# Hourglass attention and an MoE layer on one core: q and k interleaved token by token, and new prices for the order of work

## The chip, the core and the metric

The kernel runs on one core of a Trainium2 chip. Its time is the device time of one execution in microseconds. The core has five engines with a queue each, and every queue is worked off in order: TensorE (PE, with weight loads shown apart as PEld), VectorE (DVE), ScalarE (ACT), GpSimd (POOL) and SyncE (SP), which here only issues DMAs. Engines wait for each other by semaphores.

## The reference

Eight batches with eight heads, 576 tokens and 64 dimensions go through two attentions, whose outputs are added, and then through a layer with a tanh shrink:

```python
q_d, k_d, v_d = mean over 4 neighbouring tokens of q, k, v          # 144 tokens
out_up = repeat(softmax(q_d @ k_d.T / 8) @ v_d, 4)                   # full attention, pooled
scores = where(abs(i - j) < 4, q @ k.T / 8, -1e9)                    # local attention
out_local = softmax(scores) @ v
x = (out_up + out_local) as [4608 tokens, 8 heads * 64]
h = x @ w_in                                                         # 512 -> 2048
out = (h - tanh(h)) @ w_out                                          # 2048 -> 512
```

Inputs and output are float32; the kernel computes its matmuls in bf16.

## The kernel before

**Attention by pairs of heads.** The function `attention(p)` builds the work of one pair of heads; there are 32 pairs (p = 0 to 31), four to a batch. Per pair: q and k are loaded into `qkn` (two DMAs), with q on even and k on odd partitions; a cast to bf16 sorts them into `qr` (L447 on GpSimd for p >= 4); then they are transposed, so that the head dimension lies on partitions, and copied to `qk`. For p < 16 the transpose is nine matmuls on TensorE into PSUM (L477) and one ScalarE copy of 1,152 elements (L481). For p >= 16 (`T_DMA`) it is a DMA transpose `qT` issued by SP (L464) and two ScalarE copies of 576 elements, one for q, one for k (L468). `qk` is a tile of 1,192 columns: 576 of q, nine zeros, 576 of k from column `KOFF` = 585, and 31 zeros.

Two additions pool groups of four tokens (`half` L492, `qkd` L497). Local scores are eight matmuls L511 for token blocks 0 to 3 and two for block 4, each of 128 k columns against 120 (96) q columns of one head; pooled scores are four matmuls L534. Exponentials run on ScalarE (L552, L563, L566), band masks on VectorE (L556 for 960 columns, L570 for 192). Eighteen output matmuls (L581, L588) follow, then reciprocal and normalising on VectorE (L600, L602). For p < 16 the result is transposed back on TensorE (L612 to L616) and joined on VectorE (L643). For p >= 16 it is transposed by a DMA `lT` (L619) and joined (two operations, L626 and L632) on VectorE or GpSimd, whichever the planner picks. The pooled v of p >= 16 is made on GpSimd (L402, L406).

**The MoE part** works on nine blocks of 512 tokens. `mm1` (L663) makes a 128 x 512 tile of h from four matmuls, ScalarE the tanh (L671), VectorE the difference `gT` (L674). `mm2` (L690) makes 128 rows of output from sixteen matmuls; ScalarE copies them to `y` (L701), SP stores them (L704). There are 576 matmuls of each kind. Four PSUM tiles `ps_hy` are shared by both. A block needs all four pairs of every batch that it touches.

**The order** is made by a planner, the class `Program`. Each operation is recorded with an engine, an assumed duration in ns, what it reads and writes, and a priority. `order()` plays this through: whichever engine is free first takes the ready operation with the lowest priority number. Attention has 10 * p; MoE matmuls have 5000, so they fill what time is left on TensorE. Operations with a choice of engines take the one that is free first in the plan. The instructions are emitted in the planned order, and the chip then runs each engine's queue in that order, whatever the real durations are. `slack` is an extra delay that the planner may assume before an operation.

Of the kernel before, what the change touches and what calls it, by code (L numbers as in the profile page):

```python
# [184 lines left out]
def kernel(  # L185
# [18 lines left out]
    A9 = 9  # L204
# [4 lines left out]
    KOFF = 585  # L209
# [27 lines left out]
    qk = fixed("qk", [128, 1192], BF16, 2)  # L237
    qT = fixed("qT", [128, A9, 128], BF16, 2)
    half = fixed("half", [128, 2, G, 2], FP32)
# [193 lines left out]
    def attention(p):  # L433
# [8 lines left out]
        cold = 1.5 if p < NP else 1.0  # L442

# [8 lines left out]
        for h in range(2 if p < NEARLY else 0):  # L452
# [3 lines left out]
                      for eng, ns, fn in REORDER[h]],  # L456
# [4 lines left out]
        full = bass.AP(tensor=qk[s].tensor, offset=qk[s].offset,  # L461
                       ap=[qk[s].ap[0], [KOFF, 2], [1, 576]])
        if p >= T_DMA:
# [3 lines left out]
            for i in range(2):  # L467
                op("ACT", 600, lambda i=i: A.copy(  # L468
                    out=full[:, i].rearrange("p (g a) -> p g a", a=A9),
                    in_=qT[s].rearrange("p a (g i) -> p i g a", i=2)[:, i]),  # L470
                   reads=[("qT", s)], writes=[("qk", s, i)], pri=pri)
        else:
            b16 = ps.rearrange("p n c -> p (n c)").bitcast(BF16)[:, 0:2 * S]

            def tr():
# [3 lines left out]
            op("PE", 520 * cold, tr, reads=[("qr", s, 0), ("qr", s, 1), "ident"],  # L479
               writes=ts, pri=pri)  # L480
            op("ACT", 1240, lambda: A.copy(  # L481
                out=full.rearrange("p i (g a) -> p i g a", a=A9),
                in_=b16.rearrange("p (a g i) -> p i g a", a=A9, i=2)),
               reads=ts,
               writes=[("qk", s, 0), ("qk", s, 1)], pri=pri)


        four = full.rearrange("p i (g a) -> p i g a", a=4)
        adders = ADDERS[p >= NEARLY]

        def add1(eng):
            eng.tensor_tensor(out=half, in0=four[:, :, :, 0:2],  # L492
                              in1=four[:, :, :, 2:4], op=ALU.add)

        def add2(eng):
            with nc.allow_low_precision("pooled q and k"):
                eng.tensor_tensor(out=qkd[s][:, 0:2 * G].rearrange("p (i g) -> p i g", i=2),  # L497
                                  in0=half[:, :, :, 0],
                                  in1=half[:, :, :, 1], op=ALU.add)
        P.choice([(name, n1, lambda eng=eng: add1(eng)) for name, n1, _, eng in adders],  # L500
                 reads=[("qk", s, 0), ("qk", s, 1)], writes=["half"], pri=pri)
# [6 lines left out]
        def score(t, hh, c, sc=sc):  # L508
            rows = slice(64 * hh, 64 * hh + 64)
            k0 = KOFF + QW * t - 4  # L510
            T.matmul(sc[:, c:c + NQ[t]], qk[s][rows, k0:k0 + 128],  # L511
                     qk[s][rows, QW * t:QW * t + NQ[t]], start=p >= NP, stop=p >= NP or t >= 3)
# [27 lines left out]
        qks = [("qk", s, i) for i in range(2)]  # L540
# [3 lines left out]
        if new:  # L544
            op("PE", 620, s12, reads=qks + [("qkd", s)], writes=ts + ox, pri=pri)
        else:
            op("PE", 420 * cold + 600 * (p < NP), s1,
               reads=qks + ["bias"] * (p < NP), writes=ts, pri=pri)
# [3 lines left out]
        op("ACT", 870, lambda: A.activation(  # L552
            out=e1, in_=ps[:, :, 0:480], func=AF.Exp, scale=SCALE),
           reads=ts, writes=[("E", e, 0)], pri=pri)
        if p >= NP:
            op("DVE", 850, lambda: V.tensor_tensor(  # L556
# [4 lines left out]
        if not new:  # L561
            op("PE", 380 * cold + 150 * (p < NP), s2, reads=qks + [("qkd", s)], writes=ts, pri=pri)
        op("ACT", 240, lambda: A.activation(  # L563
            out=e2v, in_=ps2[:, :, 0:96], func=AF.Exp, scale=SCALE),
           reads=ts2, writes=[("E", e, 1)], pri=pri)
        op("ACT", 560, lambda: A.activation(  # L566
            out=e3, in_=ps2[:, :, 96:384], func=AF.Exp, scale=SCALE / 16.0),
           reads=ts2, writes=[("E", e, 2)], pri=pri)
        if p >= NP:
            op("DVE", 300, lambda: V.tensor_tensor(  # L570
# [24 lines left out]
        op("PE", 570 * cold, outs,  # L595
# [6 lines left out]
        op("DVE", 1010, lambda: V.tensor_tensor(  # L602
# [15 lines left out]
        if p >= X_DMA:  # L618
# [18 lines left out]
            P.choice([("DVE", 850, lambda: join(V)), ("POOL", 1450, lambda: join(GP))],  # L637
                     reads=[("lT", s)], writes=[("x", b, j)], pri=pri)
            return
        op("PE", 370 * cold, back, reads=[("ln", s)], writes=ox, pri=pri)  # L640
# [12 lines left out]
    def mm1(kb, fc):  # L653
# [12 lines left out]
        for part in range(2):  # L666
# [4 lines left out]
        op("ACT", 490, lambda: A.activation(  # L671
            out=u[us], in_=ps_hy[slot], func=AF.Tanh),
           reads=[("hy", slot)], writes=[("u", us)], pri=-1)
        op("DVE", 620, lambda: V.tensor_tensor(  # L674
# [195 lines left out]
```

The softmax here doesn't subtract the row's maximum and nothing guards it: scores larger than these inputs give would overflow.

## Time and profile before

| what | value |
|---|---|
| median of 6 runs | 345.47 us (342.51 to 348.68) |
| profiled execution, its own time | 345.01 us |
| its span, first to last instruction | 343.3 us |
| granted TensorE clock, mean | 0.988 |
| TensorE matmuls busy | 327.1 us (95%) |
| VectorE, ScalarE, GpSimd busy | 216.1, 217.1, 162.7 us |
| DMA | 56.52 MB, mean 165 GB/s |

The span is the profiled execution without what lies around it; 1.7 us lie between the two numbers. Slices are fortieths of the span (8.6 us); a digit is a busy share in tenths. A group of instructions has a line, an engine, an operation, output and inputs with their shapes and a count; behind the first bar the busy time in us and the mean duration in ns, behind the second the idle time just before and what ended it. [...] successive matmuls overlap, and their pace is read from several in a row.

### The profile page before, as it was taken

The numbers are of one execution on the slowest core, as the hardware profiler recorded it, in microseconds if no ns is written. First come the engines' busy times: TensorE is split into PE (matmuls) and PEld (weight loads), VectorE is DVE, ScalarE is ACT, GpSimd is POOL, SyncE is SP. The second block draws the span as 40 slices with busy tenths as digits, with TensorE's granted clock in tenths as the row PEclk, the third lists the DMA queues.
The fourth block names the chain that finished last, engine by engine and source line by source line (L and its number), as shares of the span: only waits on it lengthen the run. The fifth ranks groups of instructions, "written<-read, shape, count | busy, mean of one in ns | idle before, by whom it ended". The sixth has DMA issues, their size and how long they took to land.

```text
span 343.3 us, 6637 instructions
## 1 busy us (share of the span) xinstructions
PE 327.1 (95%) x2520; PEld 163.9 (48%) x2520; DVE 216.1 (63%) x341; ACT 217.1 (63%) x350; POOL 162.7 (47%) x191
## 2 busy tenths in 40 slices
PE   7978999999999999997798899999999999999995
PEld 3554555565555554443344445455444444444442
DVE  5784784388877667979988889876433433344300
ACT  3965765679879589986758779875443444344411
POOL 6775448747798629887756889441000000000000
PEclk9998999999999999999989999999999999999999
DMA  7999999998779909999999999322201000100021
GB/s 240 283 220 228 238 279 266 298 307 226 220 187 216 256 31 213 211 217 270 226 241 238 263 233 217 79 70 61 57 32 61 31 32 31 61 31 32 31 87 67
DMA packets 99213, 56.52 MB, mean 165 GB/s; under 512 B 77678, under 2 KB 86382, under 8 KB 99182
## 3 DMA queue, kind: packets, MB, share of 16 engines
q1 hardware_dynamic: 94670, 51.32, 60.5%
q0 software_dynamic: 4224, 4.19, 7.4%
q10 hardware_dynamic: 288, 0.59, 0.5%
q8 instruction: 19, 0.31, 0.4%
q14 instruction: 12, 0.10, 0.1%
HBM read 42.46 MB, written 9.44 MB: 151 GB/s over the span
## 4 chain that ended last, share of the span: by engine, by line
PE 75%; DVE 12%; ACT 6%; DMA 2%; issue 2%; POOL 1%; SPq 0%; ACTq 0%; POOLq 0%; DVEq 0%
PE ps_hy L663 31%; PE ps_hy L690 30%; DVE E L556 4%; PE ps_ox L581 3%; PE ps_ts L511 2%; DVE gT L674 2%; PE ps_ts L477 2%; PE ps_ox L588 2%; DVE xT L632 2%; DVE E L570 2%; ACT E L552 2%; DMA qkn<-in_q_dram 2%; DVE xT L626 2%; PE ps_ox L616 1%; ACT qk L468 1%
## 5 line engine op out<-in xcount | busy, mean ns | idle before, releaser
L663 PE MATMUL ps_hy<-xT,w_in_sb 128*128 128x512 bf16 x576 | 146.8, 383 | 2.2 <-DVE xT L643 1.5
L690 PE MATMUL ps_hy<-w_out_sb,gT 128*128 128x512 bf16 x576 | 144.0, 382 | 0.0
L674 DVE TENSOR_TENSOR gT<-ps_hy,u 128x512 bf16<-128x512 f32 x144 | 96.4, 684 | 73.9 <-ACT u L671 73.2
L671 ACT ACTIVATE u<-ps_hy 128x512 f32<-128x512 f32 x144 | 84.5, 601 | 69.4 <-PE ps_hy L663 68.9
L690 PEld LDWEIGHTS <-gT 128*128 128x128 bf16 x576 | 54.5, 98 | 62.5 <-issue 1.1
L663 PEld LDWEIGHTS <-w_in_sb 128*128 128x128 bf16 x576 | 53.8, 98 | 63.6 <-issue 5.0
L492 POOL TENSOR_TENSOR half<-qk 128x576 f32<-128x576 bf16 x29 | 33.6, 1158 | 30.7 <-ACT qk L481 15.6
L447 POOL CAST qr<-qkn 128x1152 bf16<-128x1152 f32 x28 | 33.5, 1197 | 11.2 <-PE ps_ts L477 5.6
L468 ACT COPY qk<-qT 128x576 bf16<-128x576 bf16 x32 | 38.1, 1215 | 0.0
L556 DVE TENSOR_TENSOR E<-E,mask 128x960 bf16<-128x960 bf16 x28 | 28.3, 1011 | 13.2 <-ACT E L552 12.8
L552 ACT ACTIVATE E<-ps_ts 128x960 bf16<-128x960 f32 x30 | 29.2, 974 | 10.3 <-PE ps_ts L511 10.0
L701 ACT COPY y<-ps_hy 128x512 f32<-128x512 f32 x36 | 21.1, 586 | 19.2 <-PE ps_hy L690 18.7
L602 DVE TENSOR_TENSOR ln<-ps_ox,r 128x896 bf16<-128x896 f32 x30 | 32.7, 1089 | 0.9
L381 POOL CAST vw<-vst 128x640 bf16<-128x640 f32 x32 | 26.1, 816 | 7.0 <-DMA vst<-in_v_dram 5.4
L581 PE MATMUL ps_ox<-vw,E 128*128 128x65 bf16 x300 | 19.4, 194 | 6.3 <-DVE E L570 4.5
L481 ACT COPY qk<-ps_ts 128x1152 bf16<-128x1152 bf16 x14 | 15.7, 1124 | 13.1 <-PE ps_ts L477 11.3
L581 PEld LDWEIGHTS <-E 128*128 128x128 bf16 x320 | 16.1, 98 | 14.1 <-DVE E L570 5.3
L402 POOL TENSOR_TENSOR v<-v 72x512 f32<-72x512 f32 x16 | 20.8, 1303 | 0.9
L497 POOL TENSOR_TENSOR qkd<-half 128x288 bf16<-128x288 f32 x29 | 20.3, 699 | 0.9
L406 POOL TENSOR_TENSOR vp<-v 72x256 bf16<-72x256 f32 x16 | 12.3, 771 | 14.2 <-PE ps_ox L588 13.2
L511 PEld LDWEIGHTS <-qk 64*128 64x128 bf16 x320 | 9.6, 95 | 17.1 <-issue 16.3
L570 DVE TENSOR_TENSOR E<-E,mask 128x192 bf16<-128x192 bf16 x28 | 15.5, 555 | 0.4 <-ACT E L563 0.3
(90 smaller groups left out, 255.2 us busy)
## 6 DMA issues: line engine op xcount, KB each, us to landing
vst<-in_v_dram SPq DMA_DIRECT2D x62, 160.0 KB, 4.9
qkn<-in_q_dram SPq DMA_DIRECT2D x32, 288.0 KB, 5.1
out_dram<-y SPq DMA_DIRECT2D x36, 256.0 KB, 2.0
qkn<-in_k_dram SPq DMA_DIRECT2D x30, 288.0 KB, 4.8
v<-in_v_dram SPq DMA_DIRECT2D x16, 288.0 KB
w_in_sb<-in_moe_w_in_dram POOLq DMA_DIRECT2D x4, 512.0 KB, 11.2
w_out_sb<-in_moe_w_out_dram POOLq DMA_DIRECT2D x4, 512.0 KB, 10.0
qkn<-in_k_dram ACTq DMA_DIRECT2D x2, 288.0 KB, 3.3
```

The costliest lines, as they stand in the source:

```text
L381: P.choice([(eng, ns, lambda fn=fn: fn(out=vw[w][:, 2 * jj:2 * jj + 2, :, 0:64], in_=vst[s])) for eng, ns, fn in CAST_V[p >= NEARLY]], rea ...
L447: op("POOL", 1300, lambda: GP.tensor_copy(out=qr[s].rearrange("p a (h d) -> p h a d", h=2), in_=qkn[sn].rearrange("p h (a d) -> p h a d", ...
L468: op("ACT", 600, lambda i=i: A.copy(out=full[:, i].rearrange("p (g a) -> p g a", a=A9), in_=qT[s].rearrange("p a (g i) -> p i g a", i=2)[: ...
L492: eng.tensor_tensor(out=half, in0=four[:, :, :, 0:2], in1=four[:, :, :, 2:4], op=ALU.add)
L552: op("ACT", 870, lambda: A.activation(out=e1, in_=ps[:, :, 0:480], func=AF.Exp, scale=SCALE), reads=ts, writes=[("E", e, 0)], pri=pri)
L556: op("DVE", 850, lambda: V.tensor_tensor(out=e1, in0=e1, in1=mask[:, 0:480].unsqueeze(1).to_broadcast([128, 2, 480]), op=ALU.mult), reads= ...
L581: T.matmul(po[:, hh, 65 * t:65 * t + 65], E[e][:, c:c + 128], vw[w][:, 2 * jj + hh, t, :], start=True, stop=True)
L602: op("DVE", 1010, lambda: V.tensor_tensor(out=ln[s].rearrange("p n (h d) -> p h n d", d=D), in0=blocks[:, :, :, 0:64], in1=r[s].unsqueeze( ...
L663: T.matmul(ps_hy[slot], w_in_sb[:, dc, fc * 128:(fc + 1) * 128], xT[dc][:, kb * 512:kb * 512 + 512], start=(dc == 0), stop=(dc == N_DC - 1))
L671: op("ACT", 490, lambda: A.activation(out=u[us], in_=ps_hy[slot], func=AF.Tanh), reads=[("hy", slot)], writes=[("u", us)], pri=-1)
L674: op("DVE", 620, lambda: V.tensor_tensor(out=gT[g][:, fc, :], in0=ps_hy[slot], in1=u[us], op=ALU.subtract), reads=[("hy", slot), ("u", us) ...
L690: T.matmul(ps_hy[slot], gT[g][:, fc, ts * 128:ts * 128 + 128], w_out_sb[:, fc, :], start=(fc == 0), stop=(fc == N_FF - 1))
```

## The change

1. `qk` becomes [128, 608, 2]: four zero tokens (`LEAD`), 576 tokens, 28 zero tokens, and for every token q and k side by side. The copies out of the transposed tile move pairs of q and k, which lie side by side in it too. For p >= 16 one copy takes the place of two. The score matmuls read every second column of `qk`. The two additions run over tokens, then q and k.
2. The planner's assumed durations are set anew: the copy 1250 in place of two of 600, exponentials 960, 310 and 650 (870, 240, 560), masks 950 and 450 (850, 300), normalising 1060 (1010), tanh and y copy 590 (490), gT 670 (620), the join 1900 on VectorE and 1400 on GpSimd (850 and 1450).
3. `M2_FIRST` goes from 16 to 12: of the first block's sixteen steps of `mm2`, twelve stand alone and four go between the second block's `mm1`.
4. New parameters: `slack=late` on TensorE's attention operations with `LATE` = 0, and `DPRI` = -1 where -1 stood.

```diff
-    KOFF = 585
+    LEAD = 4
-    qk = fixed("qk", [128, 1192], BF16, 2)
+    qk = fixed("qk", [128, LEAD + 576 + 28, 2], BF16, 2)
-    half = fixed("half", [128, 2, G, 2], FP32)
+    half = fixed("half", [128, G, 2, 2], FP32)
...
-        full = bass.AP(tensor=qk[s].tensor, offset=qk[s].offset,
-                       ap=[qk[s].ap[0], [KOFF, 2], [1, 576]])
+        full = qk[s][:, LEAD:LEAD + 576]
         if p >= T_DMA:
...
-            for i in range(2):
-                op("ACT", 600, lambda i=i: A.copy(
-                    out=full[:, i].rearrange("p (g a) -> p g a", a=A9),
-                    in_=qT[s].rearrange("p a (g i) -> p i g a", i=2)[:, i]),
-                   reads=[("qT", s)], writes=[("qk", s, i)], pri=pri)
+            op("ACT", 1250, lambda: A.copy(
+                out=full.rearrange("p (g a) i -> p g a i", a=A9),
+                in_=qT[s].rearrange("p a (g i) -> p g a i", i=2)),
+               reads=[("qT", s)], writes=[("qk", s)], pri=pri)
...
-                out=full.rearrange("p i (g a) -> p i g a", a=A9),
-                in_=b16.rearrange("p (a g i) -> p i g a", a=A9, i=2)),
+                out=full.rearrange("p (g a) i -> p g a i", a=A9),
+                in_=b16.rearrange("p (a g i) -> p g a i", a=A9, i=2)),
...
-            eng.tensor_tensor(out=half, in0=four[:, :, :, 0:2],
-                              in1=four[:, :, :, 2:4], op=ALU.add)
+            eng.tensor_tensor(out=half, in0=four[:, :, 0:2, :],
+                              in1=four[:, :, 2:4, :], op=ALU.add)
...
-                eng.tensor_tensor(out=qkd[s][:, 0:2 * G].rearrange("p (i g) -> p i g", i=2),
-                                  in0=half[:, :, :, 0],
-                                  in1=half[:, :, :, 1], op=ALU.add)
+                eng.tensor_tensor(out=qkd[s][:, 0:2 * G].rearrange("p (i g) -> p g i", i=2),
+                                  in0=half[:, :, 0, :],
+                                  in1=half[:, :, 1, :], op=ALU.add)
...
-            T.matmul(sc[:, c:c + NQ[t]], qk[s][rows, k0:k0 + 128],
-                     qk[s][rows, QW * t:QW * t + NQ[t]], start=p >= NP, stop=p >= NP or t >= 3)
+            k0, q0 = LEAD + QW * t - 4, LEAD + QW * t
+            T.matmul(sc[:, c:c + NQ[t]], qk[s][rows, k0:k0 + 128, 1],
+                     qk[s][rows, q0:q0 + NQ[t], 0], start=p >= NP, stop=p >= NP or t >= 3)
...
-        op("DVE", 300, lambda: V.tensor_tensor(
+        op("DVE", 450, lambda: V.tensor_tensor(
...
-            P.choice([("DVE", 850, lambda: join(V)), ("POOL", 1450, lambda: join(GP))],
+            P.choice([("DVE", 1900, lambda: join(V)), ("POOL", 1400, lambda: join(GP))],
...
-    M2_FIRST, T_DMA, X_DMA, NEW = 16, 16, 16, 16
+    M2_FIRST, T_DMA, X_DMA, NEW, LATE = 12, 16, 16, 16, 0
+    DPRI = -1
...
-            V.memset(qk[i][:, 576:585], 0.0)
-            V.memset(qk[i][:, 1161:1192], 0.0)
+            V.memset(qk[i][:, 0:LEAD], 0.0)
+            V.memset(qk[i][:, LEAD + 576:LEAD + 604], 0.0)
```

## The prediction

> **What bounds the kernel now.** I began with the page's busy shares and slices, to see which engine the span follows.
>
> ```profile
> PE 327.1 (95%) x2520; PEld 163.9 (48%) x2520; DVE 216.1 (63%) x341; ACT 217.1 (63%) x350; POOL 162.7 (47%) x191
> ...
> PE   7978999999999999997798899999999999999995
> ...
> DVE  5784784388877667979988889876433433344300
> ```
>
> TensorE is busy nearly everywhere, with a dent in slices 19 to 24, where VectorE is at 8 to 9 tenths. So I split the span at four marks of TensorE's timeline: its first MoE matmul (26.75), the scores of pair 16, the first with DMA transposes (122.77), the end of the last pair's output matmuls (238.38), the end. The busy time of each stretch:
>
> ```profile
> 0.00:26.75 26.75, 21.66 (x262) 13.14 (x263) 18.96 (x51) 16.59 (x26) 20.24 (x38) 1.00 1.04 246
> 26.75:122.77 96.02, 96.01 (x884) 52.09 (x884) 65.86 (x103) 70.11 (x118) 62.68 (x69) 0.98 0.99 241
> 122.77:238.38 115.61, 108.30 (x910) 52.99 (x909) 95.22 (x133) 91.60 (x139) 79.73 (x85) 0.99 0.87 191
> 238.38:343.30 104.92, 101.17 (x474) 45.68 (x470) 36.05 (x55) 38.78 (x68) 0.01 (x1) 0.99 0.13 45
> ```
>
> The columns are PE, PEld, DVE, ACT and POOL busy, then clock and DMA. The last stretch is TensorE alone: eight MoE matmuls take 1.73 us in the chain, so one takes 0.216. The order of instructions puts 396 of them into the third stretch: 85.5 us. Each pair adds 0.48 us for its fourteen score matmuls, 0.58 for its eighteen output matmuls and about 0.1 where they change over, 1.16 x 16 = 18.6. So TensorE needs 104.1 us there and takes 115.6: **11.5 us are lost**. What it waits for is in the waits of that stretch and, at one place, in the timeline:
>
> ```profile
> PEld L581 <- DVE E L570: 5.3, 6, 2.0
> PE ps_ox L581 <- DVE E L570: 4.5, 6, 1.9
> PEld L581 <- DVE E L556: 4.2, 5, 1.8
> ...
> 169.61 1.06 DVE L570 TENSOR_TENSOR E<-E,mask 128x192 bf16<-128x192 bf16 x1
> 170.73 0.20 PE L581 MATMUL ps_ox<-vw,E 128*128 128x65 bf16 x1 [1.88 <-DVE E L570]
> ```
>
> The output matmuls wait for VectorE's masks. The groups of the crowded part (122.8 to 205.9) say why VectorE is late:
>
> ```profile
> L674 DVE TENSOR_TENSOR gT<-ps_hy,u 128x512 bf16<-128x512 f32 x34 | 22.9, 682 | 5.6 <-ACT u L671 5.5
> L556 DVE TENSOR_TENSOR E<-E,mask 128x960 bf16<-128x960 bf16 x11 | 15.2, 1383 | 4.9 <-ACT E L552 4.8
> L602 DVE TENSOR_TENSOR ln<-ps_ox,r 128x896 bf16<-128x896 f32 x11 | 12.0, 1091 | 0.4
> L626 DVE TENSOR_TENSOR xT<-lT 128x480 bf16<-128x480 bf16 x6 | 7.3, 1213 | 0.3 <-DMA lT<-ln 0.3
> L632 DVE TENSOR_TENSOR xT<-lT 128x96 bf16<-128x96 bf16 x6 | 7.2, 1192 | 0.0
> L570 DVE TENSOR_TENSOR E<-E,mask 128x192 bf16<-128x192 bf16 x11 | 6.9, 628 | 0.1
> ```
>
> A pair costs VectorE 1.38 + 0.63 (masks) + 0.24 + 1.09 (normalising) + 3 x 0.68 (three gT) = 5.4 us, and the join 2.4 more for 11 pairs of 16: 7.0 on average. But the order most often puts 24 MoE matmuls into a pair, 24 x 0.216 + 1.16 = 6.34 us. VectorE cannot keep that pace, and TensorE, which takes its queue in order, waits. The planner did not see it: it priced a join at 0.85 us and a qk copy at 0.60, where the trace has 2.4 and 1.21.
>
> [...] The copy of before reads single bf16 values 256 bytes apart, and the trace agrees that this is slow:
>
> ```profile
> L468 ACT COPY qk<-qT 128x576 bf16<-128x576 bf16 x32 | 38.1, 1215 | 0.0
> ...
> L481 ACT COPY qk<-ps_ts 128x1152 bf16<-128x1152 bf16 x14 | 15.7, 1124 | 13.1 <-PE ps_ts L477 11.3
> ```
>
> Half the elements take longer from SBUF than all of them from PSUM. [...] No interleaved load is in this trace. [...] the same 192-column mask takes 0.24 us or 1.06.
>
> **The change part by part.**
>
> *The copy.* Two copies of 1.215 become one of 1,152 elements in 4-byte pairs[...]. Bounds: 1.15 (the PSUM copy) and 2.43 (no gain). I take 1.2. ScalarE is relieved of 1.2 us x 16 = 19 us, but TensorE's waits are on VectorE, so little of this is worth time directly. It keeps exponentials and tanh from being late.
>
> *Score matmuls on every second column.* [...] I take no change. Bounds: nothing, and +0.67 us a pair (rival C).
>
> *The adders.* The first reads runs of four values in place of two, at nothing. The second now writes q and k sums alternately, 288 bytes apart; 0.70 us for 288 elements could become about 1.05[...]. GpSimd's six operations of a pair (qr 1.20, two adds 1.16 and 0.70, vw 0.82, v and vp 1.30 and 0.77) then take 6.3 us at most; with one join of 1.4, two pairs take 14, under the 16.1 below.
>
> *Zero edits.* LATE is 0, so the slack arguments add nothing; DPRI is the old -1; the guard memsets stay in the lead-in.
>
> *The new prices move the order*, and this is the main term. In the new order pairs alternate between 26 and 38 MoE matmuls, and the third stretch holds 490 in place of 396 (288 become 290 before it, 468 become 372 after it; total unchanged). Two pairs get 64 x 0.216 + 2 x 1.16 = 16.1 us of TensorE. VectorE keeps 9 joins of 16 in place of 11, so two pairs need 2 x 3.34 + 8 x 0.68 + 2.4 = 14.5 us of it; ScalarE needs 2 x (1.2 + 0.97 + 0.34 + 0.67) + 8 x 0.6 + 2 x 0.59 = 12.3. All fit.
>
> Is the work also in the right places? Take the odd pair, scores at 0, output matmuls after 14 MoE matmuls at 0.48 + 3.02 = 3.50. Exponential 0.42 to 1.39, large mask to 2.8, small mask to 3.45; the fifth output matmul needs it at 3.6. The join then holds VectorE to 5.9, and two gT, the reciprocal, a gT, the normalising and a gT to 9.9; the even pair's large mask is due at 10.7. Its output matmuls come after 18 at 13.6, the masks are ready at 13.4; then come gT, reciprocal, normalising and two gT until 17.2, and the next large mask is due at 17.4. The order closes, with 0.2 to 0.8 us to spare. Masks scatter by more, so I leave 0.3 us a pair for the eleven crowded ones: about **3 us stay**. The join waits behind its lT transpose (3.2 us to landing); its cover is the 0.8 us before 10.7, and if that is gone, gT is late next, then the tanh behind its buffers.
>
> SP's order brings qT just before lT of the even pair; the qr cast that it waits for now has GpSimd's spare 2 us a cycle. Loads: in the crowded part DMA is 1.02 busy at 7.2 us a pair; at 8.05 it has a tenth more room.
>
> *The lead-in.* The fourth pair's second add moves from VectorE (1.39 us at 18.34, during a GpSimd add) to GpSimd, ahead of two weight issues and the next qr cast. The cast ends about 0.7 later, TensorE's transposes follow, then the fourth output: the first MoE matmul comes **0.7 later** (bounds -0.5 and +1). M2_FIRST 12 only holds back the last quarter of the first block's second matmuls, as filler among those of the next: nothing.
>
> Sum on the profiled execution (345.0; span 343.3 and 1.7 around it): 345.0 - 11.5 + 3.0 + 0.7 = 337.2. The median, 345.47, lies 0.5 above it, so **337.7 us**.
>
> **Rivals.**
> A. The pair copy stays at 2.43. ScalarE then has 14.8 us in 16.1, and the odd pair's exponential comes 0.2 late instead of 1.0 early; with scatter 3 us more: 341. For it: each pair still jumps 256 bytes. [...]
> B. Collisions of GpSimd and VectorE set the pace whatever the order: both stay near nine tenths, the slack is under their scatter (masks 0.66 to 2.2 us), and a third to a half of the loss stays: 341.5. Against: with GpSimd idle after 206, pairs with 24 to 32 MoE matmuls lost at most 0.3 us.
> C. Slower: interleaved columns defeat the hidden weight load. Fourteen loads and matmuls now pass in 0.38 us, while one load lasts 95 ns; seven a side in the open would cost 7 x 0.095 = 0.67 us, x 32 pairs = 21 us, on the engine that is the bound: 359. It decides from 0.35 us a pair. For it: no strided operand in the trace. [...]
>
> **How the numbers follow.** Forecast 0.65 (own range 334 to 341), A 0.10, B 0.13, C 0.09, a lead-in or DMA mishap that eats the gain 0.03. Low: no stall left and no lead-in loss, 333.9, less 0.4 for the spread of runs: 333.5. High: A, B and half-effects of C up to 344; that leaves out about 0.13. Faster by over 1% (about what can be told from no change): most of the forecast and A, half of B: 0.78. Within 1%: 0.12. Slower: C and the mishap: 0.10.
>
> **What would show it.** Right: one qk copy near 1.2 us, sixteen times; output matmuls' waits on the masks under 4 us; the pure MoE tail about 80 us in place of 101; score matmuls still 0.38 us for fourteen. Wrong: score groups of 0.7 us or more, or waits on masks near 10 us again.

## The result: no change, and the profile after

The changed kernel takes 347.38 us (median of 35 runs, 343.04 to 352.16) beside 346.33 for the kernel before (72 runs on the same chips): a ratio of 1.002, 95% interval 1.000 to 1.004. The forecast was 337.7 and faster. The profiled execution of the changed kernel took 348.38 us, 1.0 more than its median (a second one, below, 349.05), while that of before lay 1.3 below its own, so the two traces differ by more than the medians do.

The page of the changed kernel, busy shares and slices, where the kernel before was read first:

```profile
PE 325.9 (94%) x2520; PEld 164.9 (48%) x2520; DVE 217.1 (63%) x336; ACT 202.9 (59%) x334; POOL 185.6 (54%) x196
...
PE   7887999999969999898989898999999999999995
...
DVE  5865884579777676868787777776766343334300
...
PEclk9899999999998999999999999999999999999999
```

ScalarE lost 14 us of work, as the change wants. GpSimd gained 23, about ten more than the forecast has for it (0.35 us for each of 28 additions and two joins of 1.4). The dent in slices 19 to 24 is now a comb from slice 17 on (8, 9, 8, 9), and there is a new hole in slice 12, with a lower clock behind it in slice 13. The same four stretches, cut at the same events (columns as before: PE, PEld, DVE, ACT and POOL busy, clock, DMA):

```profile
0.00:30.12 30.12, 23.37 (x262) 13.89 (x262) 20.47 (x50) 17.10 (x26) 21.89 (x39) 0.94 1.05 252
30.12:130.57 100.45, 96.71 (x885) 52.70 (x884) 71.60 (x103) 68.58 (x117) 71.11 (x68) 0.98 0.90 220
130.57:262.33 131.76, 125.24 (x999) 61.90 (x999) 97.20 (x142) 86.93 (x140) 91.25 (x88) 1.00 0.78 174
262.33:346.60 84.27, 80.58 (x382) 36.41 (x378) 27.86 (x42) 30.25 (x53) 1.31 (x2) 0.99 0.13 47
```

Beside the forecast, in us of the span. The forecast's stretches are those of before, with 0.7 for the lead-in, two MoE matmuls more in the middle, 490 x 0.216 + 18.6 + 3.0 in the late stretch, and 96 matmuls fewer in the tail:

| stretch | before | forecast | after | after minus forecast |
|---|---|---|---|---|
| lead-in, to the first MoE matmul | 26.75 | 27.45 | 30.12 | +2.7 |
| pairs 4 to 15 | 96.02 | 96.45 | 100.45 | +4.0 |
| late, pairs 16 to 31 | 115.61 | 127.4 | 131.76 | +4.4 |
| MoE tail | 104.92 | 84.2 | 84.27 | +0.1 |
| span | 343.3 | 335.5 | 346.6 | +11.1 |

So the work moved as forecast, and all three crowded stretches are longer than they need be. The groups show what has changed its duration, from the page and the list of groups, first three lines of before, then the changed kernel:

```profile
L497 POOL TENSOR_TENSOR qkd<-half 128x288 bf16<-128x288 f32 x29 | 20.3, 699 | 0.9
...
L556 DVE TENSOR_TENSOR E<-E,mask 128x960 bf16<-128x960 bf16 x28 | 28.3, 1011 | 13.2 <-ACT E L552 12.8
...
L570 DVE TENSOR_TENSOR E<-E,mask 128x192 bf16<-128x192 bf16 x28 | 15.5, 555 | 0.4 <-ACT E L563 0.3
```

```profile
L495 POOL TENSOR_TENSOR qkd<-half 128x288 bf16<-128x288 f32 x30 | 46.0, 1535 | 1.8 <-DVE half L490 0.9
...
L554 DVE TENSOR_TENSOR E<-E,mask 128x960 bf16<-128x960 bf16 x28 | 32.4, 1157 | 14.8 <-ACT E L550 14.7
...
L568 DVE TENSOR_TENSOR E<-E,mask 128x192 bf16<-128x192 bf16 x28 | 21.2, 757 | 5.8 <-ACT E L561 5.7
...
L467 ACT COPY qk<-qT 128x1152 bf16<-128x1152 bf16 x16 | 19.4, 1210 | 0.0
```

The one qk copy takes 1.21 us, as forecast. The second addition, 0.70 us before, takes **1.535 us** on GpSimd and 1.84 on VectorE (the mean of two). The masks, undisturbed 0.66 and 0.25, average 1.16 and 0.76, where they averaged 1.01 and 0.56 before.

**Lead-in.** VectorE's part, first before, then after: the second addition of the first pair, and the cast to qr that queues behind it.

```profile
9.09 0.85 DVE L497 TENSOR_TENSOR qkd<-half 128x288 bf16<-128x288 f32 x1
...
10.73 0.74 DVE L455 CAST qr<-qkn 128x576 bf16<-128x576 f32 x1
```

```profile
9.25 1.88 DVE L495 TENSOR_TENSOR qkd<-half 128x288 bf16<-128x288 f32 x1
...
11.91 0.74 DVE L456 CAST qr<-qkn 128x576 bf16<-128x576 f32 x1
```

The cast is 1.2 us later, and TensorE's transposes of the next pair wait for it (1.09 us). The rest of the delay is less clear-cut: the clock is low from 14 to 18 us (0.62 and 0.53), and GpSimd has a second addition of 1.51 us ahead of the next cast, the first of p >= 4, which starts at 23.87 in place of 20.47.

**Late stretch.** The waits of 130.57 to 262.33, in us in total, times and longest:

```profile
PEld L579 <- DVE E L568: 5.5, 4, 1.4
PE ps_ox L579 <- DVE E L568: 5.0, 4, 1.2
PEld L579 <- DVE E L554: 3.0, 5, 2.0
```

They are hardly less than the 5.3, 4.5 and 4.2 of before; under 4 was forecast. From one score group to the next it takes 6.8 and 10.8 us in turn, where 6.8 and 9.4 are needed (26 and 38 MoE matmuls at 0.216, plus 1.16): the first five odd pairs lose 1.4 us each (the very first 1.8), the sixth nothing. One of them in the timeline:

```profile
174.46 1.80 DVE L554 TENSOR_TENSOR E<-E,mask 128x960 bf16<-128x960 bf16 x1 [0.17 <-ACT E L550]
176.18 1.69 DVE L568 TENSOR_TENSOR E<-E,mask 128x192 bf16<-128x192 bf16 x1
...
174.59 1.15 POOL L490 TENSOR_TENSOR half<-qk 128x576 f32<-128x576 bf16 x1
175.68 1.15 POOL L381 CAST vw<-vst 128x640 bf16<-128x640 f32 x1
176.80 1.49 POOL L495 TENSOR_TENSOR qkd<-half 128x288 bf16<-128x288 f32 x1
...
177.93 0.20 PE L579 MATMUL ps_ox<-vw,E 128*128 128x65 bf16 x1 [1.24 <-DVE E L568]
```

The large mask, 1.80 us, lasts as long as 0.66 and GpSimd's first addition (1.15) together. The small mask, 0.25 alone, starts 0.65 us before the vw cast ends and lasts 1.69, to 0.42 before the recorded end of the slow addition that follows the cast; TensorE waits 1.24 us for it. Three more odd pairs show the same (small masks of 1.69 us at 158.60, 193.76 and 211.33). In this profile the masks with no GpSimd operation beside them take 0.24 to 0.26 us (eight small ones) and 0.65 or 0.66 (nine large ones).

**Pairs 4 to 15.** The hole is one event, at pair 12:

```profile
98.57 3.16 DVE L568 TENSOR_TENSOR E<-E,mask 128x192 bf16<-128x192 bf16 x1 [1.66 <-ACT E L561]
...
98.50 0.72 POOL L406 TENSOR_TENSOR vp<-v 72x256 bf16<-72x256 f32 x1
99.18 1.48 POOL L495 TENSOR_TENSOR qkd<-half 128x288 bf16<-128x288 f32 x1
100.25 1.37 POOL L448 CAST qr<-qkn 128x1152 bf16<-128x1152 f32 x1
...
102.45 0.72 PE L420 MATMUL ps_ox<-vw,pick 128*128 128x256 bf16 x5 [2.54 <-DVE xT L641]
```

A mask of 0.25 us that arrives 0.07 us after a GpSimd operation lasts 3.16 us, through three of them in a row. The join behind it on VectorE is late, and TensorE stands still for 2.54 us. Windows of 2 us show what comes next (the number before the DMA share is the granted clock):

```profile
100.00:102.00 2.00, 0.00 (x0) 0.00 (x0) 2.00 (x2) 0.92 (x1) 2.00 (x3) 1.00 0.00 0
102.00:104.00 2.00, 1.55 (x9) 0.95 (x9) 1.37 (x2) 0.59 (x1) 1.87 (x2) 0.81 0.44 103
104.00:106.00 2.00, 2.00 (x18) 1.45 (x17) 0.35 (x1) 0.62 (x2) 0.04 (x1) 0.50 0.92 287
```

Half clock follows the stall. The missing shares of three windows, 0.19, 0.50 and 0.16 (the clock is 0.84 from 106 to 108) of 2 us each, make 1.7 us more.

### The profile page after: what moved, and what is told of

It reads as the page before. It is cut to its first block, busy times and chain, and to the rows that moved or that the text cites. A ratio compares the mean times of both kernels' runs of the same rounds, so it can differ in the third digit from the quotient of the medians.

```text
span 346.6 us, 6605 instructions
## 1 busy us (share of the span) xinstructions
PE 325.9 (94%) x2520; PEld 164.9 (48%) x2520; DVE 217.1 (63%) x336; ACT 202.9 (59%) x334; POOL 185.6 (54%) x196
## 4 chain that ended last, share of the span: by engine, by line
PE 82%; DVE 6%; DMA 3%; ACT 3%; POOL 3%; issue 1%; SPq 0%; ACTq 0%; POOLq 0%
PE ps_hy L688 34%; PE ps_hy L661 33%; DVE E L554 3%; DMA qkn<-in_k_dram 3%; PE ps_ox L579 3%; DVE E L568 3%; PE ps_ts L509 3%; PE ps_ox L586 2%; PE ps_ts L476 2%; ACT E L550 2%; PE ps_ox L420 1%; PE ps_ox L614 1%; POOL qkd L495 1%; POOL qr L448 1%; ACT u L669 1%
## 5 line engine op out<-in xcount | busy, mean ns | idle before, releaser
L688 PE MATMUL ps_hy<-w_out_sb,gT 128*128 128x512 bf16 x576 | 142.1, 379 | 0.0
L495 POOL TENSOR_TENSOR qkd<-half 128x288 bf16<-128x288 f32 x30 | 46.0, 1535 | 1.8 <-DVE half L490 0.9
L554 DVE TENSOR_TENSOR E<-E,mask 128x960 bf16<-128x960 bf16 x28 | 32.4, 1157 | 14.8 <-ACT E L550 14.7
L448 POOL CAST qr<-qkn 128x1152 bf16<-128x1152 f32 x28 | 33.7, 1204 | 13.4 <-PE ps_ts L476 10.9
L381 POOL CAST vw<-vst 128x640 bf16<-128x640 f32 x32 | 29.1, 913 | 2.4 <-PE ps_ox L579 2.0
L568 DVE TENSOR_TENSOR E<-E,mask 128x192 bf16<-128x192 bf16 x28 | 21.2, 757 | 5.8 <-ACT E L561 5.7
L624 POOL TENSOR_TENSOR xT<-lT 128x480 bf16<-128x480 bf16 x7 | 7.3, 1048 | 23.2 <-DMA lT<-ln 23.1
L467 ACT COPY qk<-qT 128x1152 bf16<-128x1152 bf16 x16 | 19.4, 1210 | 0.0
## 6 DMA issues: line engine op xcount, KB each, us to landing
w_out_sb<-in_moe_w_out_dram POOLq DMA_DIRECT2D x4, 512.0 KB, 10.9
```

The source lines that it names most:

```text
L448: op("POOL", 1300, lambda: GP.tensor_copy(out=qr[s].rearrange("p a (h d) -> p h a d", h=2), in_=qkn[sn].rearrange("p h (a d) -> p h a d", ...
L554: op("DVE", 950, lambda: V.tensor_tensor(out=e1, in0=e1, in1=mask[:, 0:480].unsqueeze(1).to_broadcast([128, 2, 480]), op=ALU.mult), reads= ...
L568: op("DVE", 450, lambda: V.tensor_tensor(out=e2v, in0=e2v, in1=mask[:, 480:576].unsqueeze(1).to_broadcast([128, 2, 96]), op=ALU.mult), rea ...
L688: T.matmul(ps_hy[slot], gT[g][:, fc, ts * 128:ts * 128 + 128], w_out_sb[:, fc, :], start=(fc == 0), stop=(fc == N_FF - 1))
```

## The experiments

Each ratio is to runs of the kernel before on the same chip, with its 95% interval. "The changed kernel" is 1.002 on this scale.

### Which part did it: four kernels

Theory 1: the second addition, whose write now jumps between the q half and the k half of `qkd`, eats the gain. Rivals: the new order by itself, or the layout's other parts.

**Pooled pairs** (the changed kernel, with `qkd` too in pairs, so that the second addition writes in a row and the pooled score matmuls read every second column; to make room, `bias` moves into `qT`):

```diff
-    qkd = fixed("qkd", [128, 344], BF16, 2)
+    qkd = fixed("qkd", [128, 200, 2], BF16, 2)
...
-  out=qkd[s][:, 0:2 * G].rearrange("p (i g) -> p g i", i=2),
+  out=qkd[s][:, 0:G],
...
-  T.matmul(sc[:, c:c + G], qkd[s][rows, k0:k0 + 128], qkd[s][rows, 0:G], ...)
+  T.matmul(sc[:, c:c + G], qkd[s][rows, k0:k0 + 128, 1], qkd[s][rows, 0:G, 0], ...)
```

> The kernel after, with one edit: the pooled q and k are kept in pairs too, so that the second addition writes a run of 288 neighbouring values instead of two streams 288 bytes apart, and the pooled score matmuls read every second column. The order of instructions is that of after. Theory 1 (the split write of the second addition ate the gain): the addition falls from 1.54 us to 0.7 to 0.9 us on GpSimd, the first MoE matmul comes near 27 us instead of 30, the waits on the masks fall, and the time is 338 to 341 us, 2 to 2.5 percent below before. Theory 2 (the new order itself brings nothing, because collisions of VectorE and GpSimd set the pace): the addition may fall, but the time stays within 1 percent of before, 345 us or more.

340.11 us, ratio 0.982 (0.977 to 0.988). The addition takes 0.70 us, the first MoE matmul comes at 27.61, and the stretches are 98.7, 127.7 and 84.3. Theory 1 holds: the addition is worth 2%. (Planes in turn, below, changes nothing but the addition, and is worth 1.2%.)

**The layout alone** (the new tile, with the old durations for the planner, `M2_FIRST` 16 and the copy in two halves, so that the order is that of before):

```diff
-            op("ACT", 1250, lambda: A.copy(... all 64 groups of nine tokens ...
+            for i in range(2):
+                op("ACT", 600, lambda i=i: A.copy(... groups 32 * i to 32 * i + 31 ...
```

> The new layout with the old prices and M2_FIRST 16, so that every engine's order is that of before; the copy from qT is made in two halves of the groups, to keep two instructions. Theory 1: the second addition costs 1.5 us and, with before's order, nothing pays for it: the lead-in is 3 us longer, and the late pairs, which were given 6.3 us each, need about 7 us of GpSimd: 351 to 356 us. Theory 2 (the addition lies beside other work): within 1 percent of before, 344 to 349 us.

352.80 us, ratio 1.022 (1.017 to 1.027). Additions of 1.60 us on GpSimd, 1.87 on VectorE. In the old order the layout is a loss.

**The durations alone** (the old layout, with two copies of 1.2 us, in the new order):

```diff
-                op("ACT", 600, lambda i=i: A.copy(
+                op("ACT", 625, lambda i=i: A.copy(
...
-            P.choice([("DVE", 850, lambda: join(V)), ("POOL", 1450, lambda: join(GP))],
+            P.choice([("DVE", 1900, lambda: join(V)), ("POOL", 1400, lambda: join(GP))],
```

(and the other new durations, with `M2_FIRST` 12)

> The old layout with the new prices and M2_FIRST 12; the two copies are priced 625 each, so that the order is nearly that of after, while each still takes 1.21 us. Theory 1: the second addition is 0.7 us as in before, VectorE and GpSimd have room, ScalarE is fuller by 19 us in all: 339 to 342 us. Theory 2 (the order brings nothing): 345 us or more.

341.48 us, ratio 0.988 (0.983 to 0.993). The new order gains 1.2% without the layout. The interval meets that of pooled pairs, so the faster copy, which came with the change of layout, could not be told from nothing.

**Pooled pairs for the first four pairs alone** (the jumping write from pair 4 on):

```diff
-  out=qkd[s][:, 0:2 * G].rearrange("p (i g) -> p g i", i=2),
+  out=(pairs in a row if p < NP else qkd[s][:, 0:2 * G].rearrange("p (i g) -> p g i", i=2)),
```

> The kernel after, with pooled q and k kept in pairs for the first four pairs of heads only. Theory 1: the lead-in alone heals, the first MoE matmul comes at 27 us instead of 30, and the time is about 3 us below after; the rest of the gap to the version with pairs throughout is what the slow addition costs later. Theory 2: the late first matmul in the profile of after was chance, and the time is that of after within 1 us.

344.99 us, ratio 0.997 (0.994 to 1.001): the lead-in is worth about half a per cent, less than expected. Most of the 2% is lost behind it, where GpSimd has time to spare (in the changed kernel it is busy for 71.1 of 100.5 us in pairs 4 to 15 and for 91.3 of 131.8 in the late stretch). How, is the next question. The profiled execution took 341.89 us, and even so the hole at pair 12 is in it: a mask of 3.16 us, a stall of 2.54, half clock.

### Is it the write, its price in the plan, or its length?

**Planes in turn** (the changed kernel, all q sums first and then all k sums: a write in a row, reads 16 bytes apart):

```diff
-  qkd[s]... "p (i g) -> p g i",  in0=half[:, :, 0, :]
+  qkd[s]... "p (i g) -> p i g",  in0=half[:, :, 0, :].rearrange("p g i -> p i g")
```

> The changed kernel, with only the loop order of the second addition turned: all 144 q sums first, then all 144 k sums, so that it writes 144 values in a row and then 144 more, and reads one float32 every 16 bytes. Theory 1 (the 288-byte jumps of the write are what costs): the addition falls from 1.54 to 0.70-0.80 us, the first MoE matmul comes near 27.6, the time is 339-342, a ratio near 0.982. Rival (it is the reading of scattered halves, too): the addition stays between 1.0 and 1.5 us, the time between 344 and 347.

341.95 us, ratio 0.990 (0.985 to 0.995).

```profile
L495 POOL TENSOR_TENSOR qkd<-half 128x288 bf16<-128x288 f32 x30 | 22.2, 741 | 3.2 <-DVE half L490 2.3
```

0.74 us with scattered reads, 1.535 with the jumping write: the write is what costs. A loop order turned round mends it. Yet at pair 12 a mask still lasts 2.50 us here, and TensorE waits 0.92 and then 1.88 us; its clock stays at 1.00.

**The honest price** (the changed kernel, with the addition as slow as it is, but the planner told so):

```diff
-    ADDERS = [[("DVE", 700, 420, V), ("POOL", 1150, 750, GP)], [("POOL", 1150, 750, GP)]]
+    ADDERS = [[("DVE", 700, 1850, V), ("POOL", 1150, 1500, GP)], [("POOL", 1150, 1500, GP)]]
```

> The changed kernel, with the planner told what the slow second addition costs (1500 on GpSimd, 1850 on VectorE in place of 750 and 420); the operations stay as they are. If the loss lies in an order made from a wrong price: most of it returns, 340-343, with the additions still at 1.5 us. If it lies in the 0.8 us themselves, on GpSimd's queue ahead of the qr cast and the masks: 345-348, as the changed kernel, within 1%.

340.56 us, ratio 0.986 (0.981 to 0.991), with additions of 1.54 us. The first MoE matmul comes at 26.93, pairs 4 to 15 take 96.3 us at full clock; the late stretch keeps its losses (130.4). A slow operation that the plan knows of costs far less than one that it doesn't. Long masks alone don't explain that: the longest small mask of all, 3.62 us, is in this trace (at 100.04), but TensorE loses only 1.49 us behind it, and its clock stays at 1.00.

**The cheap addition twice** (pooled pairs, doubled from pair 4 on):

```diff
+                for _ in range(1 + (p >= NP)):
```

> The kernel with pooled pairs (cheap second addition, 340.11), in which GpSimd does the cheap second addition twice for pairs 4 to 31: 1.40-1.45 us of GpSimd in place of 0.70, with no jumping write. Only the length matters: as the kernel with pooled pairs for the first four pairs alone, 344-346, pair 16 at 129-130. Rival (the jumping write also slows what runs beside it, VectorE's masks above all): quicker than that one, 340-342.

338.61 us, ratio 0.981 (0.976 to 0.986). I had expected 344 to 346 if length were all; twice 0.73 us on GpSimd cost nothing that can be measured. At pair 12, the place of the hole:

```profile
98.66 0.82 DVE L569 TENSOR_TENSOR E<-E,mask 128x192 bf16<-128x192 bf16 x1 [1.66 <-ACT E L562]
...
98.58 0.73 POOL L406 TENSOR_TENSOR vp<-v 72x256 bf16<-72x256 f32 x1
99.26 1.49 POOL L496 TENSOR_TENSOR qkd<-half 128x288 bf16<-128x288 f32 x2
...
100.20 0.72 PE L420 MATMUL ps_ox<-vw,pick 128*128 128x256 bf16 x5 [0.21 <-DVE xT L642]
```

The mask comes as late behind the same operation as before (0.08 us), but gets in at the next boundary. TensorE waits 0.21 us in place of 2.54, and the clock stays at 1.00.

**The changed kernel once more** (one profiled execution):

> A second profiled execution of the changed kernel, unaltered. Theory of the close race (whether VectorE's mask or GpSimd's first addition starts first is decided by about 0.1 us): the pairs' periods in the late stretch differ between two executions of the one kernel, some odd pairs near 10.8 us and some near 9.4, and the sum of the stretch differs by over 2 us. Rival (the order alone sets it): the same alternation of 6.8 and 10.8 as in the first profile, within 0.3 us a pair.

349.05 us. The hole at pair 12 is there again, with the same 3.16 us and the half clock. In the late stretch the first four odd pairs take 10.8 to 11.1 us and the rest 9.4, where it was five; the stretch takes 130.6 in place of 131.8. That is 1.1 us, not over 2: the rival is nearer, order and durations repeat the pattern. Yet the kernel with pooled pairs for the first four, with the same order and the same slow additions here, left the pattern after one odd pair in its profile (126.1 us, less than the 127.7 of pooled pairs), so it is not a fixed one either: the same slow addition can cost the late stretch some 5 us or next to nothing, and no run shows what decides.

### Four attempts at the mechanism that did not settle it

Theory 2: with the jumping write GpSimd's next instruction starts 0.42 us before the addition's recorded end (after all other operations it starts about 0.05 before), and so a mask finds no gap. Rival 2: the length of one undivided instruction.

**Slow halves** (the changed kernel; from pair 4 on, two additions of 72 groups):

```diff
+  for lo, hi in [(0, G)] if p < NP else [(0, G // 2), (G // 2, G)]:
+      eng.tensor_tensor(out=two[:, lo:hi], in0=half[:, lo:hi, 0, :], in1=half[:, lo:hi, 1, :], ...)
```

> The changed kernel, with the slow second addition of pairs 4 to 31 cut into two instructions of 72 groups each: the same jumping writes and the same sum of about 1.5 us, but a boundary between instructions in the middle. Theory 2 (with the jumping write, GpSimd's next instruction starts 0.42 us before the addition's end, so a VectorE mask that waits finds no gap and sits through two or three GpSimd instructions): the halves overlap their followers too, masks of 3 us and more stay, and the time is within 1% of the changed kernel, 345-349. Rival 2 (it is only the length of one undivided instruction): VectorE gets in at the boundary, no mask over 2.9 us, and the time is that of the twice-added kernel plus its lead-in loss, 340-343.

342.88 us, ratio 0.992 (0.988 to 0.996). Halves of 0.99 us on average, 1.49 the two together since they overlap; the next operation starts 0.42 before their end, and yet there is no mask over 2.6 us. Theory 2 fails. At pair 12 TensorE waits only 0.92 and 0.53 us in a row, and even so its clock is 0.57 in the next 4 us, so this kernel keeps part of the loss. Its profiled execution (345.35 us) also has another loss, a wait of 2.93 us at 65 us for the weights `w_out_sb` to land; the changed kernel's profile has none.

**One long addition** (pooled pairs; one instruction that computes the values twice):

```diff
+  if p >= NP: the access patterns get an outer step of two; the second copy goes to unused columns
```

> The kernel with pooled pairs, with the second addition of pairs 4 to 31 made one instruction of twice the length: it computes its 288 values twice, into two places, with no jumping writes, near 1.40 us. Theory 2 (the overlap of the jumping write keeps VectorE out, not length): no overlap over 0.1 us with the next GpSimd instruction, and the time near the twice-added kernel, 338-342. Rival 2 (length of one instruction): masks of 3 us and more, and 343-347.

343.68 us, ratio 0.990 (0.987 to 0.993). It took 1.20 us, not the expected 1.40, overlaps nothing, and yet a small mask of 2.95 us at pair 12 leads to a wait of 2.3 us and to half clock. Against theory 2 again. But rival 2 is no law either: the kernel with planes in turn has masks of 2.5 to 3.1 us with additions of 0.74. What such a mask sits through is a run of GpSimd operations back to back, and at which boundary it gets in I could not derive.

**No mask at pair 12** (the changed kernel without the one mask that was caught; that pair's last block is left unmasked):

```diff
-  V.tensor_tensor(out=e2v, in0=e2v, in1=mask..., op=ALU.mult)
+  V.memset(E[e][:, 1150:1152], 1.0) if p == 12 else V.tensor_tensor(...)
```

> The changed kernel, which leaves out the 192-column mask of pair 12 (VectorE sets two columns in its place, without reading); the rest, slow additions and order, stays. Theory 3 (in pairs 4 to 15 the loss of the slow addition is one event: this mask sits 3.16 us behind GpSimd's queue, TensorE stands still for 2.5 us, and its granted clock is 0.5 for some 3 us after that): the stall and the low clock near 104 go, pair 16 starts 4 us earlier (some 126-127 at a first MoE matmul of 30), the time falls by 3.5-4.5, to 343-344, a ratio near 0.990. Rival (the next mask is caught in the same way, or the work is late by GpSimd's longer queue itself): within 1 us of the changed kernel.

351.16 us, ratio 1.018 (1.012 to 1.025): slower, not faster. The hole at pair 12 is gone, and pair 14 has one in its place. Its mask, TensorE's wait and the window behind it:

```profile
116.38 6.74 DVE L554 TENSOR_TENSOR E<-E,mask 128x960 bf16<-128x960 bf16 x1 [0.17 <-ACT E L550]
...
125.05 0.29 PE L611 MATMUL ps_ox<-ident,ln 128*128 128x128 bf16 x1 [4.40 <-DVE ln L601]
...
124.00:126.00 2.00, 0.95 (x8) 0.81 (x9) 1.53 (x2) 0.00 (x0) 1.42 (x2) 0.50 1.26 213
```

A mask of 0.66 us lasted 6.74, through a row of GpSimd operations without a gap, and half clock followed for more than 5 us. One event taken out let the next one in, so the theory of a single event falls; stall and clock it shows again. (2.4 us of a wait for `w_out_sb` at 63 us are in this trace as well.)

**No small masks late** (the same, and the small masks of pairs 16 to 31 left out too):

```diff
+  small = p == 12 or p >= 16
```

> As the kernel without pair 12's small mask, and it also leaves out the small masks of pairs 16 to 31 (two columns set instead). Theory 3 continued (the late stretch loses 5 to 7 us because VectorE's masks lose the race against GpSimd's first addition every second pair): the odd pairs go back to 9.4 us, the late stretch is 127-128 in place of 131-133, and the time 338-340, a ratio near 0.978, with all additions still slow. Rival (GpSimd's 0.8 us more a pair, not the collisions, hold the late pairs): odd pairs stay near 10.8, the time that of the kernel without pair 12's mask.

348.38 us, ratio 1.013 (1.006 to 1.019), with the same 6.74 us at pair 14. The late stretch takes 127.6 us, inside the expected 127 to 128, but two odd pairs still stand at 10.9 to 11.1, since the large masks are caught as well. The total misses mostly by what pair 14 costs, 4.4 us of stall and 3.4 of clock.

### All masks out: what the collisions are worth

The two kernels differ as the changed kernel and pooled pairs do, and neither has a mask from pair 4 on (local attention is unmasked there).

```diff
-  V.tensor_tensor(out=e1, in0=e1, in1=mask..., op=ALU.mult)      # and e2v likewise
+  V.memset(E[e][:, 0:2], 1.0)
```

**Slow addition:**

> The changed kernel, which leaves out both masks of pairs 4 to 31 (VectorE sets two columns instead, without reading), so that nothing of VectorE's in front of the output matmuls can be held up by GpSimd. The slow additions and the order stay. If the masks' collisions with GpSimd are how the slow addition costs TensorE anything behind the lead-in: no odd pair over 9.4 us, no half clock behind a mask, the late stretch near 125, a time within 3 us of the same kernel with the cheap addition, 337-340. If GpSimd's longer queue costs by itself (qr casts and pooled v late): 342-346, 4 us or more above the same kernel with the cheap addition.

**Cheap addition, pooled pairs:**

> The kernel with pooled pairs (cheap second addition), which leaves out the same masks. The pair to compare with the kernel without masks and with the slow addition: with masks the two lie 6.8 us apart (347.4 and 340.1 against their kernels before). Collisions theory: without masks they lie 2-3 us apart, the lead-in's part alone, this one at 335-337. Queue theory: still 5-7 us apart.

337.41 us, ratio 0.980 (0.975 to 0.985), and 335.88, ratio 0.978 (0.972 to 0.984). With masks the two kernels lie 2.0% apart; without masks 0.15%, within the intervals (1.5 us between the medians), though the addition still takes 1.53 us in the first and 0.68 in the second. Pairs 4 to 15 and the late stretch, first with the slow addition, then with the cheap one:

```profile
29.82:128.80 98.98, 96.55 (x886) 52.12 (x886) 54.42 (x103) 68.41 (x117) 69.91 (x68) 0.98 0.93 222
128.80:253.13 124.33, 124.33 (x999) 61.75 (x999) 73.96 (x142) 87.03 (x140) 89.03 (x88) 1.00 0.82 188
...
28.88:125.61 96.73, 95.06 (x885) 51.68 (x885) 54.43 (x103) 68.36 (x117) 60.15 (x68) 1.00 0.98 232
125.61:250.03 124.42, 124.42 (x999) 61.80 (x999) 74.43 (x142) 86.91 (x140) 79.18 (x88) 1.00 0.81 186
```

In the late stretch TensorE is busy all the time in both, and with the slow addition the six odd pairs that took 10.8 or 9.4 now all take 9.4. This settles the matter there: GpSimd's longer queue by itself (casts and pooled v that come later) costs TensorE nothing. What the slow addition costs comes by way of VectorE's masks, or of VectorE work that has less room with them: the masks' own 0.9 us a pair went too, in both kernels alike, and no run tells these two apart.

For pairs 4 to 15 it is not settled. The two profiles still lie 2.25 us apart there, no less than with masks (100.45 and 98.7). No stall behind VectorE is left in either. But with the slow addition this stretch starts with half clock (0.50 and 0.67 from 30 to 34 us; the other profile has its low clock in the lead-in) and has a wait of 1.51 us for `w_out_sb`, 0.28 in the other. Those weights are issued from GpSimd's queue, the last of them 0.8 us later with the slow addition, so its longer queue can have a part in that.

### A kernel that beats both

**Pooled pairs in the honest order, and honest prices for four pairs.** The first is the kernel with pooled pairs (0.70 us really), ordered with 1500 and 1850 in the plan. The second is the changed kernel with these prices for pairs 0 to 3 alone.

```diff
+    ADDERS = [[("DVE", 700, 1850, V), ("POOL", 1150, 1500, GP)], [("POOL", 1150, 1500, GP)]]   # first
+    ADDERS = [[("DVE", 700, 1850, V), ("POOL", 1150, 1500, GP)], [("POOL", 1150, 750, GP)]]    # second
```

> The kernel with pooled pairs (cheap second addition, really 0.70 us), in the order that the planner makes when told 1500 and 1850. The two gains add where they lie in different stretches: first MoE matmul at or before 26.9, pair 16 by 123, late stretch as with pooled pairs (128 us or less): 335-338, a ratio of 0.970-0.978. If they are one and the same gain, taken twice: 340-341, ratio 0.982-0.986.

> The changed kernel, with the honest prices of the second addition (1500 and 1850) for pairs 0 to 3 alone; later pairs keep 750. If the honest order gained in the lead-in alone (26.9 in place of 30.1): 343-345. If it gained in pairs 4 to 15 alone: 346-348 as the changed kernel. If both came from the first four pairs, because everything behind them is placed anew: 340-342.

The first takes **334.69 us**, ratio **0.967** (0.963 to 0.972): a median a little under the expected 335 to 338, and the two gains add. The second takes 345.73, ratio 0.996 (0.993 to 1.000): a first MoE matmul at 28.02, and the hole at pair 12 again, so the later pairs' prices matter too. The stretches of the first:

```profile
0.00:26.96 26.96, 22.69 (x259) 13.66 (x262) 17.47 (x50) 17.01 (x27) 19.54 (x38) 1.00 1.06 259
26.96:122.15 95.19, 93.77 (x871) 51.28 (x886) 70.18 (x104) 68.51 (x117) 61.70 (x68) 1.00 0.99 238
122.15:248.14 125.99, 123.67 (x982) 61.81 (x1000) 93.94 (x142) 86.88 (x140) 81.53 (x88) 1.00 0.80 182
```

The clock is 1.00 in all three, the longest wait listed for its matmuls is 1.3 us, and the late stretch is 1.6 us above its need. Why a plan with a price that is too high for this kernel suits it so well is not isolated.

## Why the prediction was wrong

**The step that failed is "the adders".** It took the second addition from 0.70 to about 1.05 us. Measured: 1.535 on GpSimd, 1.81 and 1.88 on VectorE. Nothing measured stood behind the 1.05: no row in the trace of before has such a write. The kernel with planes in turn shows that reads 16 bytes apart cost 0.04 us here, and the jumping write 0.83.

**It then went into the sum at the wrong place.** I compared it with GpSimd's load (14 of 16.1 us in two pairs) and let it cost nothing. The load was indeed no limit: the cheap addition twice is free, and so is the slow one in the late stretch without masks. What it touches is VectorE's masks. In the trace of before a mask of 0.24 us took 1.06 beside one GpSimd addition, and I counted with one mask against one such operation. The runs also show masks that last through the rest of a cast and most of the slow addition behind it (1.69 us), through three operations in a row (3.16) and through more (6.74).

Term by term:

- *Copy:* right, 1.21 us against 1.2, which was my estimate between the bounds of 1.15 and 2.43. Rival A is out. Its worth in time was rightly put at little.
- *Score matmuls:* right. Fourteen start at 130.57 and the next MoE matmul at 131.07, 0.50 us against 0.48. That interleaved columns change nothing was my estimate, which the trace of before could not show. Rival C is out.
- *The order:* the need of the late stretch was right to 0.1 us: 490 x 0.216 + 18.6 = 124.4 against 124.33 without masks. "About 3 us stay" is right where the addition is cheap (127.7 - 124.4 = 3.3 with pooled pairs) and wrong in the changed kernel's profile: 131.8 - 124.4 = 7.4. (With pooled pairs for the first four alone, and slow additions in this stretch, the profile has 126.1 - 124.4 = 1.7.)
- *Lead-in:* +0.7 is right with pooled pairs (+0.9). In the changed kernel it is +3.4 (+2.8 in its second profile): two second additions lie on VectorE ahead of a first addition and a cast, on the path, and their price was not counted there. The low clock from 14 to 18 us has a part in the 3.4 that is not separated.
- *Pairs 4 to 15:* costed at no more than two matmuls, and +4.4 came. The stall of 2.5 at pair 12 and 1.7 of clock behind it are about as much, but the sum does not close that simply. The kernel before has 1.7 us of low clock of its own at the start of this stretch (0.95, 0.50 and 0.70 from 26 to 32), which in the changed kernel's profile fell into the lead-in. And pooled pairs, without that stall, still take 98.7, which is 2.3 above the forecast. So about 2 us there come with the new order and not with the addition; 0.92 of them is a wait for an exponential at pair 12 that the kernels with pooled pairs, durations alone and planes in turn have too.
- *The clock* had no term. The traces have 0.50 behind the stalls of 2.54 and 4.40 us, and 1.00 behind those of 1.2 in the late stretch. But the length of the wait alone does not decide: 0.92 and 0.53 us in a row had 0.57 behind them (slow halves), 0.92 and 1.88 had 1.00 (planes in turn). What decides, no run shows. In the kernel before, too, the 1.88 us at 170.73 that the prediction shows is followed by 0.79, 0.50 and 0.86 from 170 to 176: 1.7 of the 11.5 us that it counted as lost to waits were clock.
- *Tail:* right, 84.3 us where 84.2 follows from 96 matmuls fewer.
- *Rival B* named the right pair of engines, with 341.5 as its worst. It let the collisions stay as they were; the addition made them worse, so its bound was too low, and no slow rival was built on the addition. The range ended at 344 for that reason.

With the failed term mended the forecast stands nearly as made: pooled pairs take 340.1 us, 2.4 above it, with 27.6, 98.7, 127.7 and 84.3 where 27.45, 96.45, 127.4 and 84.2 were forecast. That the honest order takes 334.7, 3.0 below it, is luck as far as the forecast goes: it knew nothing of that order.

## What to carry to other kernels

When a layout changes, price the write side of every operation that touches it, and if no row of the trace shows that access, run it alone before believing any sum; turning a loop round (planes in turn) was worth 1.2% here. An operation that is off the critical path is not free if one on another engine lasts longer beside it, as the masks did here (0.25 us alone, 1.69 and 3.16 beside GpSimd's operations): ask which short operation on TensorE's path comes up behind it, not only whether its engine has time. And tell a planner what a changed operation costs, since an order made from 0.75 us for 1.5 cost 1.6% here (1.002 against 0.986).

## What the runs showed of the hardware

- A write of bf16 values that alternates between two places 288 bytes apart: 288 values take 1.535 us in place of 0.70 on GpSimd. On VectorE they take 1.81 and 1.88 in the changed kernel and 1.48 at the least (the honest price), in place of 0.46 to 1.39 before; waiting for GpSimd may be in some of these. Reads every 16 bytes with a write in a row: 0.74 on GpSimd.
- Masks on VectorE lasted through several GpSimd operations back to back: one of 0.25 us took 3.16, one of 0.66 took 6.74. With a lag of 0.07 to 0.08 us behind the same operation it got in after one (cheap addition twice) or after three (changed kernel).
- Behind a stall of TensorE of 2.54 us at pair 12 the granted clock fell to 0.50 in both profiles of the changed kernel. Read as time at exactly half, the missing shares make 3.4 us in the first (2 x 1.7) and 6.8 in the second (0.84, 0.50, 0.50, 0.50 and 0.95 in the windows of 2 us from 100 to 110); they make 6.8 behind the stall of 4.4, and 3.4 behind 0.92 and 0.53 us in a row (0.57 over 4 us). Waits of 0.92 and 1.88 in a row in the same place (planes in turn), of 0.92 and 0.21 (cheap addition twice) and of 1.49 (the honest price) left it at 1.00.
- Score matmuls whose columns lie 4 bytes apart take what packed ones take (0.50 us against 0.48 for fourteen).
